# Wo in two parts: twelve split matmuls with the masked sums, the third modulation behind them, and w1's pieces split later

## The chip, the cores and the metric

The kernel runs on one core of one Trainium2 chip. The metric is the device time of one execution in microseconds (us). Before the change it is 433.62 us, the median of 3 runs (433.53 to 434.19).

A core has five engines, each of which works through its own list of instructions: TensorE (PE, matrix products, which write to PSUM), ScalarE (ACT), VectorE (DVE), GpSimd (POOL) and SyncE (SP). SP and POOL also issue transfers (DMA). In the profile, PEld is PE loading the stationary operand.

## What is computed

One block of a network over S = 2048 tokens of D = 448 channels: linear attention, then a mixer MLP over the tokens (F = 1792), each behind a layernorm that six vectors made from `c` modulate.

```python
x = A_x
mod = (_silu(c) @ w_mod).reshape(c.shape[0], 6, 1, -1)
sa, ca, ga, sb, cb, gb = (mod[:, 0], mod[:, 1], mod[:, 2], mod[:, 3], mod[:, 4], mod[:, 5])
h = _layernorm(x, axis=-1) * (1 + ca) + sa
x = x + ga * _A_ref(h, A_wqkv, A_wo)
h = _layernorm(x, axis=-1) * (1 + cb) + sb
x = x + gb * _B_ref(h, B_w1, B_b1, B_w2, B_b2)
```

Inside `_A_ref`, with 16 heads of 28 channels and `phi(t) = where(t > 0, t + 1, exp(t)) + 1e-6`:

```python
kv = jnp.einsum("bhsd,bhse->bhde", pk, v)
z = jnp.einsum("bhsd->bhd", pk)
num = jnp.einsum("bhqd,bhde->bhqe", pq, kv)
den = jnp.einsum("bhqd,bhd->bhq", pq, z)[..., None] + 1e-6
o = num / den            # then o, heads side by side, @ wo
```

The kernel multiplies kv by Wo before it meets the queries, so that per token only one product with a 448 x 448 matrix is left. `ga`, the third modulation vector (`mods[2]` in the code), scales the columns of that matrix.

## The kernel before

**Number format.** Most products are split: each operand is a high part, rounded to the format fp32r, and a low part, the rest. A product is then three fast matmuls: high x high, high x low and low x high. `split` (L82) makes the two parts with an ACT copy (L83) and a DVE subtraction (L84). A second way, used for some tiles, takes the subtraction off DVE: ACT copies the high part, ACT writes its negative into the low tile, and a transfer that adds, issued on POOL, puts the full value on top (`PIECE_DMA` pieces of w1 at L324 to L328; the keys' low part at L527 and L528). A few products are plain fp32 and not split: `kvb` (L818), the transposes (L863) and, before the change, Wo's product `wp` (L968).

**Order.** The schedule is written out by hand: every engine does its instructions in the order in which the code issues them, and a wait blocks what stands behind it on that engine. Tiles come from pools of buffers (`slot`: 74; `tslot`: 27; PSUM: 8 banks), and a new tile waits until the last user of its buffer is done.

**First loop** (L682 to L780, turns t = 4 to 15, one token tile of 128 rows each): keys of tile t on PE (`kp`), their exp and relu on ACT (L446, L449), `pk` on DVE (L458). `pk` of the tile before is cut into `pkh` (ACT, L515) and `pkl`; for tiles 13 to 15 `pkl` comes from DVE (L525), and `pk` is added to a running sum (L534). The normed x of one or two tiles (`HIGH_AT`) is made on DVE (`xn`, L496) and cut into `xh` (ACT, L500) and `xl` (DVE, L505, L506). PE adds the outer product of tile t - 4 into four banks `cacc` (L554), eleven matmuls a tile; the last four tiles follow behind the loop (L789 to L796). In turns 10 to 14 some query tiles are projected too (`qp`, `eq`, `rq`, `pq`). At the end of turns 13, 14 and 15 DVE multiplies parts 0, 1 and 2 of Wo (112 rows each) by `mods[2]` (L779); part 3 follows at L791.

**Behind the loop:** the sum of `pk` is closed (L784), cut into `zh` and `zl` (L786), and summed over the partitions on PE (`zp`, L799); ACT copies it to `zb`. `split_to(n)` cuts w1's pieces up to n, 0 to 7, at L794 (to 2), L803 (4), L812 (6) and L825 (8), all by `split`. From `cacc` and `zb` come four tiles `csum` (ACT L808, DVE L809). PE multiplies them with Wv (`kvb`, L818, 16 small fp32 matmuls, 32 records), DVE masks the heads' blocks (`kvm`, L822), and PE projects one more query tile (L962). Meanwhile DVE makes the denominators of tile 0: `b_prod`, `b_sum`, `b_eps` (POOL), `b_recip`, `b_scale` (L963).

**Wo's product** (L966 to L977): for each of four groups g of 112 channels one fp32 matmul of `kvm`'s columns with Wo's part g, an ACT copy out of PSUM (`wpg`, L970), and transfers that bring the rows to tiles of 128 (`Wpr`, L977). `wp_split` (L980) cuts those into `Wph` and `Wpl`.

**Second loop** (L988 to L1072): in turn i PE transposes the scaled queries of tile i (`tq`, L863), multiplies those of tile i - 1 by `Wph` and `Wpl` (`op`, L893, L900), and from turn 5 on adds up the mixer's first product (`up`, L950 to L952), which uses piece k of w1 from turn k + 5 on. Turn 0 projects three query tiles (`QS`). At the end of each turn `split_to` cuts more pieces, and `split_end` (L315) issues the adding transfers that wait. Behind it lies the rest of the MLP, which the change doesn't touch.

Of the kernel before, what the change touches and what calls it, by code (L numbers as in the profile page):

```python
# [16 lines left out]
NT = S // P  # L17
# [3 lines left out]
DH = 28  # L21
EPS = 1e-5

PIECE_DMA = range(8, 18)
PRE_LOAD = {14: 2, 15: 4}
KV_LAG = 4
HIGH_AT = {13: (11, 12), 14: (13,), 15: (14, 15)}
# [10 lines left out]
CUT2 = {2: 9, 3: 9, 4: 8, 5: 7}  # L38
LAG = 5
MOD_AT = {11: [(4, 0), (4, 1), (4, 2)], 13: [(4, 3), (4, None), (3, 0), (3, 1)]}  # L40
QS = {0: 3}
WARM = 6
POOL_LOW = (0, 1, 2)
# [8 lines left out]
def block_kernel(ctx: ExitStack, tc: tile.TileContext, x, xt, wqkv, wo, w1, b1, w2, c, wmod, wfirst, out):  # L52
# [19 lines left out]
    def tslot(name, dt=F32, parts=P, w=D):  # L72
        return tok.tile([parts, w], dt, name=name, tag="tok", padded_shape=[P, 512])


    def moving(new, name, dt=F32R, parts=P):
        return new(name, dt=dt, parts=parts, w=512)[:, 16:16 + D]

    def bank(name):
        return psum.tile([P, 512], F32, name=name, tag="bank")  # L80

    def split(full, hi, lo):  # L82
        nc.scalar.activation(hi, full, AF.Copy)  # L83
        nc.vector.tensor_sub(lo, full, hi.bitcast(F32))  # L84
# [400 lines left out]
    def a_phi_q(keep=0):  # L485
        a_exp_q(keep)
        for t in sorted(eqs):
            pq[t] = phi_q(t)
# [28 lines left out]
    def a_pk_parts(t):  # L517
        if t not in pks:
            a_pk_high(t)
        a_pk_low(t)  # L520
# [156 lines left out]
    low()  # L677
    sum_end()
    a_split(7)
    wo_sb = []  # L680
    late = [t for t in range(NT) if t not in Q_EARLY.values()]
    for t in range(4, NT):  # L682
        if 5 < t < NT - 1:
            project(t + 1, 1, "kp")
        kp = close(t, 1) if t > 4 else kps[4]
        if t == 9:
            row_sum(0)
            row_bias(0)
        if t > 4:
            a_outer(t - KV_LAG)  # L690
        if t % 2 and 4 < t < NT - 2:
            a_transpose(t + 1)
# [24 lines left out]
        a_pk_parts(t - 1)  # L717
        highs = HIGH_AT.get(t, (t - 2,))
        for i in highs[:1]:
            a_norm(i)  # L720
            a_high(i)
        if t % 2 == 0 and 4 < t < NT - 3:
            low = a_rows(t + 2)
        if t == 11:
            low2 = mod_high(2)
        for j, i in MOD_AT.get(t, ()):
            mod_add(j) if i is None else mod_part(j, i)
        if t == 14:
            low4()
        a_pk(t, kp)  # L730
        if t % 2 == 0 and 4 < t < NT - 3:
            low()
        if 7 < t + 3 < NT:
            a_split_low(t + 3)
        for i in highs[1:]:
            a_norm(i)
            a_high(i)
        if pair:
            first(1)
        for i in highs:  # L740
            a_low(i)
        if pair:
            second(1)
            end()
        sum_end()
        if 4 <= t < 8:
            w_high(0, t - 4)
            if t == 7:
                w_row(0)
        if t == 9:  # L750
            row_out(0)
        if t == 12:
            mod_out(2, mp)
            make_mask()
        if t in FETCH:
            load_xt(FETCH[t])
            load_x(FETCH[t])
        if 7 <= t < 11:
            mod_part(2, t - 7)
        if t == 10:  # L760
            mod_add(2)
        if t == 11:
            low2()
        if t == 13:
            low4 = mod_high(4)
        if t in (7, 10):
            load_mod(4 if t == 7 else 3)
        if t == 10:
            load_qkv(2, tslot)
        if t == 8:  # L770
            for g in range(4):
                w = tslot(f"wo{g}", parts=G)
                nc.sync.dma_start(w, wo[g * G:(g + 1) * G, :])
                wo_sb.append(w)
            b12 = cst.tile([P, NF + NT], F32, name="b12")
            nc.sync.dma_start(b12, b1)
            b1c, b2c = b12[:, :NF], b12[:, NF:]
        if t >= 13:
            nc.vector.tensor_mul(wo_sb[t - 13], wo_sb[t - 13], mods[2][:G])  # L779
        load_to(PRE_LOAD.get(t, 0))  # L780


    a_pk_parts(NT - 1)
    nc.vector.tensor_add(pksum[1], pksum[1], pksum[0])  # L784
# [12 lines left out]
    zp = bank("zp")  # L797
    for i, pk in enumerate(zs):
        nc.tensor.matmul(zp[:, :D], ones_r, pk, start=(i == 0), stop=(i == 1))  # L799
# [22 lines left out]
    nc.vector.tensor_mul(kvm, kvb[:G, :D], mask)  # L822
# [7 lines left out]
    pns, phs, ys, opb, sums, nms, nm2s, rss, vss = {}, {}, {}, {}, {}, {}, {}, {}, {}  # L830

    dens, prods, lasts = {}, {}, {}

    def b_prod(t):
# [13 lines left out]
    def b_scale(t):  # L848
        pn = pns.pop(t, None) or tslot(f"pn{t}", w=512)
        nc.vector.scalar_tensor_tensor(pn[:, :D].rearrange("p (h d) -> p h d", d=DH),  # L850
                                       pq[t].rearrange("p (h d) -> p h d", d=DH), 1e-6,
                                       dens.pop(t).unsqueeze(2).to_broadcast([P, H, DH]),
                                       op0=ALU.add, op1=ALU.mult)
        pns[t] = pn
        pq[t] = None

    def b_transpose(t):
        pn = pns.pop(t)
# [101 lines left out]
            del parts[k]  # L960

    a_q(late.pop(0))  # L962
    for fn in (b_prod, b_sum, b_eps, b_recip, b_scale):  # L963
        fn(0)
    mod_add(3)
    for g in range(4):  # L966
        wp = bank(f"wp{g}")
        nc.tensor.matmul(wp[:G, :D], kvm[:, g * G:(g + 1) * G], wo_sb[g], start=True, stop=True)  # L968
        wpg = tslot(f"wpg{g}", parts=G)
        nc.scalar.activation(wpg, wp[:G, :D], AF.Copy)  # L970
# [416 lines left out]
```

## Time and profile before

| what | value |
|---|---|
| median of 3 runs | 433.62 us (433.53 to 434.19) |
| the profiled execution | 434.09 us, its span 432.4 us |
| granted TensorE clock | 1.000 |
| PE busy | 427.9 us, 99% of the span |
| DVE busy | 365.1 us, 84% |
| ACT busy | 278.9 us, 65% |
| POOL busy | 120.1 us, 28% |
| Wo's product on PE (`wp`) | 3.01 us of the chain, from 108.81 us |

The span runs from the first to the last instruction on the core; the execution's own time is 1.7 us longer. A row of a timeline gives the start, the time from start to end, the engine, the line, the operation, the tile written and the tiles read, the shape and how many were merged; in brackets stands how long the engine had been idle and what ended that. Instructions of an engine overlap a little, so that one of 0.58 us can be followed by the next after 0.48. The ends of matmuls are modelled; their starts tell the rate. A row of the chain gives the start, the time on the chain, the engine, tile, line and count.

### The profile page before, as it was taken

The page shows a single profiled execution, that of the slowest core. Times are in us where ns is not written, and L with a number is a line of the kernel's source. Part 1 is how long each engine was busy: PE and PEld are TensorE (multiplying, and loading weights), DVE is VectorE, ACT ScalarE, POOL GpSimd, SP SyncE. Part 2 cuts the span into 40 slices and gives each one's busy share as a digit, 9 for nine tenths or more (in the row PEclk, how much of TensorE's full clock was granted, in tenths as well). Part 3 has the DMA queues.
Part 4 walks back from the last instruction along what each step waited for, and adds up shares of the span by engine and source line. Part 5 has one row for each costly group of instructions (what it writes and reads, how often), then busy time and mean ns, then how long its engine had stood idle before and what let it go on. Part 6 is the DMA issues. An engine that isn't in the chain of part 4 may idle for free.

```text
span 432.4 us, 7216 instructions
## 1 busy us (share of the span) xinstructions
PE 427.9 (99%) x2331; PEld 398.0 (92%) x2331; DVE 365.1 (84%) x814; ACT 278.9 (65%) x595; POOL 120.1 (28%) x199
## 2 busy tenths in 40 slices
PE   8999999999999999999999999999999999999997
PEld 8888899999899999999999999999999999999996
DVE  4899987889899999998579695739799998898894
ACT  5799869658578899996755263537464664655550
POOL 4345444300026577775200000010113131132010
PEclk9999999999999999999999999999999999999999
DMA  8997997565300036354427461577379977986431
GB/s 282 385 337 162 239 264 162 89 206 193 86 1 0 26 74 148 74 125 97 145 85 244 142 212 50 166 203 210 79 193 214 207 159 159 214 170 144 85 46 41
DMA packets 63797, 66.14 MB, mean 153 GB/s; under 512 B 4816, under 2 KB 55312, under 8 KB 63760
## 3 DMA queue, kind: packets, MB, share of 16 engines
q1 hardware_dynamic: 54688, 50.90, 37.8%
q0 software_dynamic: 8784, 14.32, 20.8%
q10 hardware_dynamic: 288, 0.46, 0.4%
q8 instruction: 18, 0.29, 0.3%
q14 instruction: 19, 0.16, 0.1%
HBM read 46.30 MB, written 7.34 MB: 124 GB/s over the span
## 4 chain that ended last, share of the span: by engine, by line
PE 97%; DVE 1%; ACT 1%; issue 0%
PE y L1183 19%; PE up L951 10%; PE up L950 10%; PE up L952 10%; PE y L1184 9%; PE cacc L554 7%; PE qp L432 7%; PE op L893 7%; PE kp L432 6%; PE op L900 1%; PE warm L188 1%; PE tq L863 1%; PE qp L439 1%; PE kvb L818 1%; PE wp L968 1%; PE rowb L287 1%
## 5 line engine op out<-in xcount | busy, mean ns | idle before, releaser
L950 PE MATMUL up<-h2h,ph 128*128 128x448 f32 x224 | 81.2, 362 | 0.0
L951 PE MATMUL up<-h2l,ph 128*128 128x448 f32 x224 | 81.2, 362 | 0.0
L952 PE MATMUL up<-h2h,pl 128*128 128x448 f32 x224 | 80.8, 361 | 0.0
L1138 POOL DMA_DIRECT2D a<-a x16 | 14.2, 964 | 142.6 <-DMA pr<-in_B_w_dram 76.7
L950 PEld LDWEIGHTS up<-h2h,ph 128*128 128x128 f32 x224 | 42.0, 188 | 3.1
L952 PEld LDWEIGHTS up<-h2h,pl 128*128 128x128 f32 x224 | 41.9, 187 | 3.0
L951 PEld LDWEIGHTS up<-h2l,ph 128*128 128x128 f32 x224 | 42.0, 188 | 2.3
L84 DVE TENSOR_TENSOR pl<-pr,ph 128x512 fp32r<-128x512 f32 x46 | 30.7, 688 | 2.6 <-ACT ph L83 1.7
L1189 ACT ACTIVATE cc<-y 128x448 f32<-128x448 f32 x24 | 13.0, 546 | 26.7 <-PE y L1184 26.7
L1102 DVE TENSOR_TENSOR u<-u,mod 128x448 f32<-128x448 f32 x14 | 8.7, 623 | 23.0 <-ACT u L1101 22.8
L83 ACT ACTIVATE ph<-pr 128x512 fp32r<-128x512 f32 x46 | 27.6, 623 | 0.8 <-PE up L952 0.5
L1101 ACT ACTIVATE u<-up,b 128x448 f32<-128x448 f32 x14 | 8.8, 625 | 25.4 <-PE up L952 24.9
L432 PE MATMUL kp<-wh,hh 128*128 128x448 f32 x64 | 23.8, 377 | 0.0
L554 PE MATMUL cacc<-pkh,xh 128*128 128x448 f32 x64 | 23.6, 369 | 0.0
L432 PE MATMUL qp<-wh,hh 128*128 128x448 f32 x64 | 23.5, 368 | 0.0
L1203 POOL DMA_DIRECT2D out_dram<-yt x14 | 12.7, 909 | 37.3 <-DVE yt L1194 27.9
L843 POOL TENSOR_SCALAR den<-den 128x16 f32<-128x16 f32 x16 | 8.8, 548 | 44.2 <-DVE den L840 44.2
L554 PE MATMUL cacc<-pkl,xh 128*128 128x448 f32 x56 | 20.3, 362 | 0.0
L893 PE MATMUL op<-wph,pth 128*128 128x448 f32 x48 | 18.7, 390 | 0.0
L1144 DVE TENSOR_TENSOR a<-a,s 128x512 f32<-128x512 f32 (+1 forms) x32 | 18.5, 622 | 0.0
L83 ACT ACTIVATE s2h<-s 128x512 fp32r<-128x512 f32 (+1 forms) x16 | 8.3, 569 | 15.5 <-DVE s L1144 15.5
L1183 PE MATMUL y<-ub,a11h 128*128 128x448 f32 x56 | 18.2, 375 | 0.0
(235 smaller groups left out, 1383.7 us busy)
## 6 DMA issues: line engine op xcount, KB each, us to landing
pr<-in_B_w_dram SPq DMA_DIRECT2D x56, 256.0 KB, 3.1
a<-in_B_w_dram SPq DMA_DIRECT2D x32, 256.0 KB, 4.8
a<-in_B_w_dram SPq DMA_DIRECT2D x32, 192.0 KB, 4.7
xt<-in_xt_dram SPq DMA_DIRECT2D x16, 256.0 KB, 5.0
x<-in_A_x_dram SPq DMA_DIRECT2D x16, 224.0 KB, 5.0
wm<-in_B_wmod_dram SPq DMA_DIRECT2D x16, 196.0 KB, 5.2
out_dram<-x SPq DMA_DIRECT2D x14, 224.0 KB, 2.3
out_dram<-yt POOLq DMA_DIRECT2D x14, 224.0 KB, 6.1
```

Source lines behind the costliest of these rows:

```text
L83: nc.scalar.activation(hi, full, AF.Copy)
L84: nc.vector.tensor_sub(lo, full, hi.bitcast(F32))
L432: nc.tensor.matmul(pps[t, j][:, :D], a[:, ch * P:(ch + 1) * P], w, start=first, stop=False)
L554: nc.tensor.matmul(cacc[ch][:, :D], a[:, s], b, start=(t == 0 and i == 0), stop=(t == NT - 1 and i == len(todo) - 1))
L893: nc.tensor.matmul(opb[t][:, :D], a, b, start=(ch == n == 0), stop=False)
L950: nc.tensor.matmul(ps[:, :D], hi[:, sl], mh, start=first, stop=False)
L951: nc.tensor.matmul(ps[:, :D], hi[:, sl], ml, start=False, stop=False)
L952: nc.tensor.matmul(ps[:, :D], lo[:, sl], mh, start=False, stop=last)
L1138: nc.gpsimd.dma_start(w, a, accum_op=ALU.add)
L1144: nc.vector.tensor_tensor(w, raw2[q, a][i], raw2[q, b][i], op=op)
L1183: nc.tensor.matmul(ps[:, :D], h[:, s], w, start=opens and r == 0, stop=False, skip_group_check=True)
L1184: nc.tensor.matmul(ps[:, :HD], l[:, s], wh, start=False, stop=closes and r == PAIRS - 1, skip_group_check=True)
```

## The change

Wo is no longer multiplied by `mods[2]` on the way in. Its four parts are cut into a high and a low tile by two activations on ACT and an adding transfer on POOL's queue, parts 0 and 1 at the end of turn 13, part 2 of turn 14 and part 3 of turn 15. `kvm` is cut as well (ACT and DVE). The four fp32 matmuls become twelve split ones, groups 0 and 1 taken in turns. DVE multiplies their results by `mods[2]` on the way out of PSUM, in place of ACT's copies.

The first tile's denominators move ahead of `kvm`, the helper functions with them. `mod_out(4)`, an ACT copy, moves ahead of `kvm`. Pieces 4 to 7 of w1 were cut at L812 and L825; now piece 4 is cut ahead of the twelve matmuls in the order of the code, piece 5 behind them, and pieces 6 and 7 at the end of turn 0 of the second loop, in the second way (two activations and a POOL transfer).

```diff
-PIECE_DMA = range(8, 18)
+PIECE_DMA = range(6, 18)
...
+WO_AT = {13: (0, 1), 14: (2,), 15: (3,)}
...
+    def wo_split(g):
+        full, hi, lo = wo_sb[g], moving(slot, f"woh{g}", parts=G), moving(slot, f"wol{g}", parts=G)
+        nc.scalar.activation(hi, full, AF.Copy)
+        nc.scalar.activation(lo, hi.bitcast(F32), AF.Copy, scale=-1.0)
+        nc.gpsimd.dma_start(lo, full, accum_op=ALU.add)
+        wos.append((hi, lo))
...
-        if t >= 13:
-            nc.vector.tensor_mul(wo_sb[t - 13], wo_sb[t - 13], mods[2][:G])
+        for g in WO_AT.get(t, ()):
+            wo_split(g)
         load_to(PRE_LOAD.get(t, 0))
...
-    nc.vector.tensor_mul(wo_sb[3], wo_sb[3], mods[2][:G])
...
     a_q(late.pop(0))
-    split_to(6)
+    b_prod(0)
+    b_sum(0)
+    b_eps(0)
     mp = mod_sum2(4)
...
     a_phi_q()
+    b_recip(0)
+    mod_out(4, mp)
     kvm = slot("kvm", parts=G)
     nc.vector.tensor_mul(kvm, kvb[:G, :D], mask)
-    mod_out(4, mp)
+    b_scale(0)
+    kvh, kvl = slot("kvh", dt=F32R, parts=G), slot("kvl", dt=F32R, parts=G)
+    split(kvm, kvh, kvl)
     load_to(PRE + MID + 3)
-    split_to(8)
...
     a_q(late.pop(0))
-    for fn in (b_prod, b_sum, b_eps, b_recip, b_scale):
-        fn(0)
     mod_add(3)
+    split_to(5)
+    wps = [bank(f"wp{g}") for g in range(4)]
+    for gs in ((0, 1), (2,), (3,)):
+        for i, (a, b) in enumerate(((kvh, 0), (kvh, 1), (kvl, 0))):
+            for g in gs:
+                nc.tensor.matmul(wps[g][:G, :D], a[:, g * G:(g + 1) * G], wos[g][b], start=(i == 0), stop=(i == 2))
     for g in range(4):
-        wp = bank(f"wp{g}")
-        nc.tensor.matmul(wp[:G, :D], kvm[:, g * G:(g + 1) * G], wo_sb[g], start=True, stop=True)
         wpg = tslot(f"wpg{g}", parts=G)
-        nc.scalar.activation(wpg, wp[:G, :D], AF.Copy)
+        nc.vector.tensor_mul(wpg, wps[g][:G, :D], mods[2][:G])
...
     low3 = mod_high(3)
+    split_to(6)
```

More of the change, by code (lines that the diff above doesn't have):

```diff
@@ L679, in block_kernel @@
     a_split(7)
-    wo_sb = []
+    wo_sb, wos = [], []
+    def wo_split(g):
[4 more added lines that the diff above has]
+        wos.append((hi, lo))
     late = [t for t in range(NT) if t not in Q_EARLY.values()]
@@ L777, in block_kernel, with b_prod, b_sum, b_eps @@
             b1c, b2c = b12[:, :NF], b12[:, NF:]
-        if t >= 13:
-            nc.vector.tensor_mul(wo_sb[t - 13], wo_sb[t - 13], mods[2][:G])
+        for g in WO_AT.get(t, ()):
+            wo_split(g)
         load_to(PRE_LOAD.get(t, 0))
+    pns = {}
+    dens, prods, lasts = {}, {}, {}
+    def b_prod(t):
+        prods[t] = tslot(f"pd{t}")
+        nc.vector.scalar_tensor_tensor(prods[t], pq[t], 1e-6, zb, op0=ALU.add, op1=ALU.mult)
+    def b_sum(t):
+        dens[t] = small.tile([P, H], F32, name=f"den{t}", tag="den")
+        nc.vector.tensor_reduce(dens[t], prods.pop(t).rearrange("p (h d) -> p h d", d=DH), axis=AX.X, op=ALU.add)
+    def b_eps(t):
+        nc.gpsimd.tensor_scalar_add(dens[t], dens[t], 1e-6)
+    def b_recip(t):
+        nc.vector.reciprocal(dens[t], dens[t])
+    def b_scale(t):
+        pn = pns.pop(t, None) or tslot(f"pn{t}", w=512)
+        nc.vector.scalar_tensor_tensor(pn[:, :D].rearrange("p (h d) -> p h d", d=DH),
+                                       pq[t].rearrange("p (h d) -> p h d", d=DH), 1e-6,
+                                       dens.pop(t).unsqueeze(2).to_broadcast([P, H, DH]),
+                                       op0=ALU.add, op1=ALU.mult)
+        pns[t] = pn
+        pq[t] = None
     a_pk_parts(NT - 1)
@@ L820, in block_kernel @@
     a_phi_q()
+    b_recip(0)
+    mod_out(4, mp)
     kvm = slot("kvm", parts=G)
     nc.vector.tensor_mul(kvm, kvb[:G, :D], mask)
-    mod_out(4, mp)
+    b_scale(0)
+    kvh, kvl = slot("kvh", dt=F32R, parts=G), slot("kvl", dt=F32R, parts=G)
+    split(kvm, kvh, kvl)
     load_to(PRE + MID + 3)
-    split_to(8)
     Wpr, Wph, Wpl = [], [], []
     H2h, H2l = [None] * NT, [None] * NT
-    pns, phs, ys, opb, sums, nms, nm2s, rss, vss = {}, {}, {}, {}, {}, {}, {}, {}, {}
-    dens, prods, lasts = {}, {}, {}
-    def b_prod(t):
-        prods[t] = tslot(f"pd{t}")
-        nc.vector.scalar_tensor_tensor(prods[t], pq[t], 1e-6, zb, op0=ALU.add, op1=ALU.mult)
-    def b_sum(t):
-        dens[t] = small.tile([P, H], F32, name=f"den{t}", tag="den")
-        nc.vector.tensor_reduce(dens[t], prods.pop(t).rearrange("p (h d) -> p h d", d=DH), axis=AX.X, op=ALU.add)
-    def b_eps(t):
-        nc.gpsimd.tensor_scalar_add(dens[t], dens[t], 1e-6)
-    def b_recip(t):
-        nc.vector.reciprocal(dens[t], dens[t])
[L848 to L855, printed above, removed]
+    phs, ys, opb, sums, nms, nm2s, rss, vss = {}, {}, {}, {}, {}, {}, {}, {}
     def b_transpose(t):
```

## The prediction

> **What bounds the kernel now.** I read the page first, its busy shares and the chain that ended last:
>
> ```profile
> PE   427.9 (99%) x2331; PEld 398.0 (92%) x2331; DVE 365.1 (84%) x814; ACT 278.9 (65%) x595; POOL 120.1 (28%) x199
> ...
> PE 97%; DVE 1%; ACT 1%; issue 0%
> ```
>
> TensorE (PE) is the chain almost from end to end, so the time moves only by what PE has more or less to do, and by new gaps in PE. Next I read the chain in order of time where the change sits:
>
> ```profile
> 98.82 2.00 PE qp L432 x10
> ...
> 106.58 2.02 PE qp L432 x10
> 108.60 0.20 PE qp L439
> 108.81 3.01 PE wp L968 x8
> 111.82 0.33 PE tq L863 x3
> ```
>
> PE runs from one group into the next. The four products with Wo (`wp`, eight records) take 3.01 us, and the next group starts the moment they end. A split matmul of the same 448 columns (`qp`) takes 2.00/10 = 0.20 us.
>
> Third, the timelines of PE, ScalarE (ACT) and VectorE (DVE) from 80 to 99 us, the last turns of the loop over the token tiles (t = 13, 14, 15). First ACT:
>
> ```profile
> 80.01 0.58 ACT L515 ACTIVATE pkh<-pk 128x448 fp32r<-128x448 f32 x1
> 80.62 0.58 ACT L527 ACTIVATE pkl<-pkh 128x448 fp32r<-128x448 f32 x1
> 81.11 1.03 ACT L500 ACTIVATE xh<-xn 128x448 fp32r<-128x448 f32 x2
> ...
> 82.50 0.62 ACT L465 ACTIVATE eq<-qp,mv 128x448 f32<-128x448 f32 x1
> ...
> 84.57 0.58 ACT L515 ACTIVATE pkh<-pk 128x448 fp32r<-128x448 f32 x1
> 86.80 0.58 ACT L500 ACTIVATE xh<-xn 128x448 fp32r<-128x448 f32 x1 [1.65 <-DVE xn L496]
> 87.28 0.62 ACT L465 ACTIVATE eq<-qp,mv 128x448 f32<-128x448 f32 x1
> ...
> 89.36 0.59 ACT L515 ACTIVATE pkh<-pk 128x448 fp32r<-128x448 f32 x1
> 91.66 0.58 ACT L500 ACTIVATE xh<-xn 128x448 fp32r<-128x448 f32 x1 [1.71 <-DVE xn L496]
> 92.61 0.58 ACT L500 ACTIVATE xh<-xn 128x448 fp32r<-128x448 f32 x1 [0.38 <-DVE xn L496]
> 93.10 0.56 ACT L515 ACTIVATE pkh<-pk 128x448 fp32r<-128x448 f32 x1
> 96.28 0.58 ACT L83 ACTIVATE zh<-pk 128x448 fp32r<-128x448 f32 x1 [2.62 <-PE cacc L554]
> ```
>
> ACT idles 1.65 + 1.71 + 0.38 + 2.62 = 6.36 us here, and the last turn's `zh` waits too. DVE shows what these waits are:
>
> ```profile
> 85.18 0.63 DVE L525 SCALAR_TENSOR_TENSOR pkl<-pk,pkh 128x448 fp32r<-128x448 f32 x1 [0.88 <-ACT pkh L515]
> ...
> 86.26 0.51 DVE L496 TENSOR_SCALAR xn<-x,mv 128x448 f32<-128x448 f32 x1
> ...
> 89.98 0.62 DVE L525 SCALAR_TENSOR_TENSOR pkl<-pk,pkh 128x448 fp32r<-128x448 f32 x1 [0.24 <-ACT pkh L515]
> ...
> 92.57 0.55 DVE L506 TENSOR_TENSOR xl<-xn,xh 128x384 fp32r<-128x384 f32 x1
> ...
> 93.84 0.62 DVE L779 TENSOR_TENSOR wo<-wo,mod 112x448 f32<-112x448 f32 x1
> 94.37 0.62 DVE L525 SCALAR_TENSOR_TENSOR pkl<-pk,pkh 128x448 fp32r<-128x448 f32 x1
> ...
> 95.56 0.63 DVE L784 TENSOR_TENSOR pk<-pk,pk 128x448 f32<-128x448 f32 x1
> 96.89 0.63 DVE L84 TENSOR_TENSOR zl<-pk,zh 128x448 fp32r<-128x448 f32 x1 [0.70 <-ACT zh L83]
> ```
>
> The two engines pass one chain back and forth: `pkh` on ACT ends 84.57 + 0.58 = 85.15, DVE's `pkl` starts at 85.18, `xn` ends 86.77, ACT's `xh` starts at 86.80. ACT's idle time is DVE working on what ACT gave it; it isn't spare. Last, what PE asks for:
>
> ```profile
> 93.86 0.36 PE L554 MATMUL cacc<-pkh,xh 128*128 128x448 f32 x1
> ...
> 94.26 0.36 PE L554 MATMUL cacc<-pkh,xl 128*128 128x448 f32 x1
> ...
> 96.26 0.36 PE L554 MATMUL cacc<-pkl,xh 128*128 128x448 f32 x1
> ...
> 98.46 0.36 PE L799 MATMUL zp<-zl,ones_r 128*128 128x448 f32 x1
> ```
>
> `xh` of tile 14 is there at 91.66 + 0.58 = 92.24 and taken at 93.86: slack 1.62. Its `xl`, ready at 93.12, is taken at 94.26: slack 1.14. `pkl` of tile 15, ready 94.99, taken 96.26: 1.27. `zl`, ready 97.52, taken 98.46: 0.94. These four slacks decide the case.
>
> **The change, part by part.**
>
> *Twelve matmuls for four.* Each split matmul is put at 0.20 us, the `qp` step (same 448 columns, 112 rows instead of 128), so 12 x 0.20 = 2.4 us for 3.01: PE has 0.6 us less. The bounds are 0.20 and the old record's 3.01/8 = 0.376 us, which gives 4.5 us and a loss of 1.5; I take 0.20, since each split group of this width in the chain steps so. The Trainium skill (FP8 and Floating Point Precision, section TensorE Precision Notes) counts four passes for a true FP32 product; sixteen passes against twelve would save, as an estimate, 4 x 0.20 = 0.8 us instead, while the trace has eight records of 0.376 us.
>
> *Wo's parts.* Eight activations, in pairs: a high part, and a negated copy of it that must wait for it. The same pair stands at 80.01 and 80.62, and the next instruction starts at 81.11: 1.10 us a pair. Two pairs stand behind turn 13 (before the `eq` at 82.50), one behind turn 14 (before the `eq` at 87.28), one behind turn 15 (before the `pkh` at 93.10). Each is last in its turn, so all of the next turn's ACT work is queued behind it. The four adding transfers go out on POOL's queue:
>
> ```profile
> 109.78 0.29 POOL L843 TENSOR_SCALAR den<-den 128x16 f32<-128x16 f32 x1 [26.39 <-DVE den L840]
> ```
>
> POOL is idle for 26.39 us up to that point, and the parts are wanted at 108.8: nothing.
>
> How far that pushes things: the chain of turn 14 starts 2.2 us late, and so does turn 15's, with 1.1 more: 3.3 us. Every link down to `xh` of tile 14 waits on ACT, so all of it passes on.
> - `xh` of tile 14: 92.24 + 3.3 = 95.54, PE wants it at 93.86: late by 1.7.
> - `xl` of tile 14: 93.12 + 3.3 = 96.42, wanted at 94.26: late by 2.2.
> - `pkh` of tile 15, with the fourth pair: 93.10 + 4.4 = 97.50, ends 98.06. DVE has lost its product with Wo (93.84) and starts `pkl` at once, 98.10 to 98.72, wanted at 96.26: late by 2.5.
> - The sum of `pk` (L784) starts 95.56 - 94.37 = 1.19 behind that `pkl`: 99.29, ends 99.92; `zh` starts 0.09 later as now, 100.01; `zl` 0.61 behind it, 100.62, ends 101.25, wanted at 98.46: late by 2.8.
>
> The lateness doesn't add up, for each stall of PE postpones the next demand; the largest, 2.8 us, is what PE has lost when `zp` ends. Nothing behind gives it back, since PE is without gaps from there on. Bounds of a pair: below, 0.96 us, two steps of 0.48 as between `xh` at 86.80 and the `eq` at 87.28, which makes the last item 2.8 - 4 x 0.14 = 2.2; above, a part's buffer that isn't free when ACT comes to it. No row shows that; with the shortest wait of ACT above, 0.38 us, at each of the four pairs it would be 2.8 + 1.5 = 4.3. I keep 1.10, the rows of the same operation.
>
> *DVE's four products with Wo removed* (0.62 us each, L779 and L791): one of them is the 0.5 us already used above; the others stood beside waits. Nothing more.
>
> *The masked sums' split.* `kvm` becomes `kvm`, `kvh` (ACT), `kvl` (DVE), with the old first-tile steps ahead:
>
> ```profile
> 106.68 0.63 DVE L822 TENSOR_TENSOR kvm<-kvb,mask 112x448 f32<-112x448 f32 x1 [0.24 <-issue]
> 107.22 1.28 DVE L84 TENSOR_TENSOR pl<-pr,ph 128x512 fp32r<-128x512 f32 x2
> ...
> 110.40 0.62 DVE L850 SCALAR_TENSOR_TENSOR pn<-pq,den 128x448 f32<-128x448 f32 x1
> ```
>
> PE covers this with a projection, 106.58 to 108.81. `kvm` ends 107.31, `kvh` (0.58) about 107.95, so 0.85 us of slack. `kvl`, behind the scaling (0.62), ends about 108.6, and the first matmul with it is the fifth, wanted at 109.6. Ahead of `kvm` DVE loses the low parts of pieces 4 and 5 (1.28 us for two) and gets the first tile's product and sum (0.62 each, as the scaling) and a small reciprocal, which waits for POOL's 0.29: by my estimate up to 0.4 us later against PE, and slack is left in both: nothing. Without that cover it would cost what is over, up to 1.2 us for the two steps.
>
> *The third modulation on DVE* instead of ACT's copies. DVE takes 0.63 us from PSUM (`kvm`'s row) against this:
>
> ```profile
> 109.60 0.55 ACT L970 ACTIVATE wpg<-wp 112x448 f32<-112x448 f32 x1 [2.45 <-PE wp L968]
> ...
> 114.92 1.16 DVE L84 TENSOR_TENSOR wpl<-wpr,wph 128x448 fp32r<-128x448 f32 x2 [0.28 <-ACT wph L83]
> ...
> 119.26 0.37 PE L893 MATMUL op<-wpl,pth 128*128 128x448 f32 x1
> ```
>
> The results leave perhaps 1 us later, behind `mod_add`, one piece's low part and each other. The first use of `wpl` is at 119.26 and it is ready near 115.5: 3.7 us of slack, nothing.
>
> *Pieces of w1.* Pieces 4 and 5 go from before `kvm` to around `wp`; 6 and 7 to the end of turn 0 of the second loop, by two activations each and a POOL transfer. Piece k is first used in turn k + 5, far off. Four activations of about 0.58 us, 2.3 us, then stand in front of turn 1, where ACT now waits:
>
> ```profile
> 119.25 0.49 ACT L871 ACTIVATE pth<-tq 128x384 fp32r<-128x384 f32 x1 [1.63 <-PE tq L863]
> ```
>
> The 0.7 us over goes into `pth`, whose next use on PE is a turn later: nothing.
>
> **Sum.** +2.8 - 0.6 = +2.2 us. The profiled execution took 434.09 us (a span of 432.4, and 1.7 around it), 0.47 over the median; on it 436.3, on the median of 433.62 it is **435.8 us**, 0.5% slower.
>
> **Rivals.**
>
> *The eight activations hide* (not slower). If ACT could put them into its 6.36 us of idle time, of which they need 4.4, PE sees nothing and the time is 433.62 - 0.6 = 433.0. For it: the totals. Against it: the waits are links of one chain, and ACT takes its instructions as written. It decides at 1.14 us, the slack of `xl` of tile 14: pairs that push it by less cost nothing there. The Trainium skill (PSUM — Partial Sum Buffer, section Engine vs sequencer instructions) calls ScalarE's and VectorE's queues strict FIFO; by that rule this rival falls, and the rows of 85 to 87 us, where ACT waits for `xn` with later work at hand, agree. Chance 0.13.
>
> *The masked sums come late as well.* If DVE is 1 us further behind than I count, `kvh` misses `wp` by 0.6: 436.4. For it: DVE is the busiest helper (84% on the page), and its two rows at 106.68 and 107.22 follow each other without a gap. Against: the slack of 0.85. Chance 0.12.
>
> *The split products aren't short* (the change doesn't do what it says): 0.376 us each, 435.8 + 2.1 = 437.9. Against it: every such row here. Chance 0.02.
>
> **How the numbers follow.** The forecast has 0.70; 0.03 remains for something that I don't see and that is faster. The range takes the low bound of a pair (2.2 - 0.6 = +1.6, 435.2), the second rival and most of the way to the buffers' bound (437.3), with half a microsecond below for slack that I read too small: 434.7 to 437.2. It leaves out the first rival and the third. 0.2% is 0.87 us, about what a measurement of this kernel can tell from no change. The first rival, at -0.14%, is "same", less a little for the case that part of the stall is left: same 0.13, slower 0.84, faster 0.03.
>
> **What would show it.** Right: PE idle before the `cacc` matmuls of tiles 14 and 15 and before `zp`, released by DVE's `xl`, `pkl` and `zl`, 2.8 us together; `zp` near 101.2 instead of 98.4; ACT's `eq` of turn 14 near 84.7 and of turn 15 near 90.6; twelve `wp` matmuls in 2.4 us, with no wait before them. Wrong: `cacc` without gaps up to `zp`, the new activations lying in ACT's old idle times, or a stall at `wp` larger than the one at `cacc`.

## The result, and the profile after

The changed kernel takes 441.5 us (median of six runs, 440.23 to 442.36) against 433.82 for the kernel before on the same chip: a ratio of 1.0176, interval 1.0157 to 1.0195. Slower, as forecast, but by 7.7 us where 2.2 was forecast, and outside the range. Two executions of the experiments below, at a granted clock of 0.558 (705.59 us, in e8) and 0.757 (526.34 us, in e18), are left out. The profiled execution took 440.93 us, with a span of 439.2. Its page, busy shares and the chain that ended last:

```profile
PE 429.1 (98%) x2335; PEld 395.7 (90%) x2335; DVE 364.1 (83%) x813; ACT 283.7 (65%) x602; POOL 126.0 (29%) x205
...
PE 76%; ACT 7%; DVE 7%; DMA 7%; issue 2%; POOL 0%; SPq 0%; ACTq 0%; DVEq 0%; POOLq 0%
```

PE is busy for 1.2 us more than before, and the span is 6.8 us longer: nearly all of the loss is waiting. The chain, 97% PE before, now runs through ACT, DVE and DMA for 21%. Where PE waits stands in its timeline (start, duration, engine, line, operation; in brackets the idle time ahead of it and what ended it):

```profile
95.50 0.47 PE L555 MATMUL cacc<-pkh,xh 128*128 128x448 f32 x1 [1.92 <-ACT xh L501]
...
96.39 0.47 PE L555 MATMUL cacc<-pkh,xl 128*128 128x448 f32 x1 [0.21 <-DVE xl L507]
...
101.37 0.37 PE L433 MATMUL qp<-wh,hh 128*128 128x448 f32 x1
...
107.22 2.61 PE L854 MATMUL kvb<-cs,wr 128*112 128x112 f32 x24 [0.24 <-DVE cs L843]
...
112.67 0.66 PE L983 MATMUL wp<-woh,kvh 112*112 112x448 f32 x2 [0.62 <-ACT kvh L84]
...
115.19 0.49 PE L877 MATMUL tq<-ident,pn 128*128 128x128 f32 x3
...
128.59 0.44 PE L914 MATMUL op<-wph,pth 128*128 128x448 f32 x1 [1.76 <-ACT rq L467]
...
129.47 0.55 PE L877 MATMUL tq<-ident,pn 128*128 128x128 f32 x3 [0.23 <-DVE pn L811]
...
134.97 0.63 PE L877 MATMUL tq<-ident,pn 128*128 128x128 f32 x4 [0.33 <-DVE pn L811]
```

The reader is to see four places, not one: at `cacc` (token tiles 14 and 15, behind the loop), from `kvb` to `wp`, at the late product of the second loop (L914, the last quarter of a tile's product with Wo, called the late `op` below), and at the transposes `tq` behind it.

The moment at which a kernel reaches this stretch differs between the traces: the query projection ahead of the last K tile starts at 84.83 us before, at 84.01 to 85.08 in three traces of the changed kernel, and at 83.77 to 85.70 in all. So all times below are counted from that projection, and given as their difference to the kernel before. The third row is a later execution of the changed kernel, not edited:

| us behind the kernel before | projection behind `zp` | projection behind `kvb` | `wp` | first `tq` | late `op` | first `up` | end |
|---|---|---|---|---|---|---|---|
| before, absolute | 13.83 | 21.52 | 23.82 | 26.82 | 38.24 | 57.67 | 347.57 |
| changed | +3.15 | +3.69 | +4.46 | +3.98 | +5.96 | +7.34 | +7.24 |
| changed, e13 | +2.74 | +3.27 | +4.03 | +3.58 | +4.00 | +5.39 | +5.35 |

From the first `up` on hardly anything is lost or won (0.1 us). ScalarE's timeline has the start of it; the single row below it is `cs` in the kernel before, without a wait:

```profile
82.47 0.56 ACT L685 ACTIVATE woh<-wo 112x448 fp32r<-112x448 f32 x1
83.07 0.58 ACT L686 ACTIVATE wol<-woh 112x448 fp32r<-112x448 f32 x1
...
84.63 0.62 ACT L466 ACTIVATE eq<-qp,mv 128x448 f32<-128x448 f32 x1
...
90.50 0.62 ACT L466 ACTIVATE eq<-qp,mv 128x448 f32<-128x448 f32 x1
...
103.79 0.64 ACT L842 ACTIVATE cs<-cacc,col 128x448 f32<-128x448 f32 x1 [0.64 <-PE qp L440]
...
105.81 1.68 ACT L842 ACTIVATE cs<-cacc,col 128x448 f32<-128x448 f32 x3 [1.38 <-PE qp L433]
...
112.04 0.58 ACT L84 ACTIVATE kvh<-kvm 112x448 fp32r<-112x448 f32 x1 [2.01 <-DVE kvm L860]
```

```profile
100.34 2.21 ACT L808 ACTIVATE cs<-cacc,col 128x448 f32<-128x448 f32 x4
```

`eq` of turn 14 starts at 84.63 (forecast 84.7) and of turn 15 at 90.50 (90.6). But `cs`, which reads only finished sums, waits for PE's query projections, first for 0.64 and then for 1.38 us. An instruction that doesn't read `qp` and waits for it is waiting for a buffer: in the built program `cs` got buffers of the split query tiles 5 and 6, which the projections were still reading; in the kernel before, the first three got buffers of K's last tile.

### The profile page after: what moved, and what is told of

Read it like the earlier page. It is cut to its first block, busy times and chain, and to the rows that moved or that the text cites. A ratio compares the mean times of both kernels' runs of the same rounds, so it can differ in the third digit from the quotient of the medians.

```text
span 439.2 us, 7243 instructions
## 1 busy us (share of the span) xinstructions
PE 429.1 (98%) x2335; PEld 395.7 (90%) x2335; DVE 364.1 (83%) x813; ACT 283.7 (65%) x602; POOL 126.0 (29%) x205
## 3 DMA queue, kind: packets, MB, share of 16 engines
HBM read 46.30 MB, written 7.34 MB: 122 GB/s over the span
## 4 chain that ended last, share of the span: by engine, by line
PE 76%; ACT 7%; DVE 7%; DMA 7%; issue 2%; POOL 0%; SPq 0%; ACTq 0%; DVEq 0%; POOLq 0%
PE y L1200 19%; PE up L965 10%; PE up L964 10%; PE up L966 10%; PE y L1201 9%; PE op L907 5%; PE cacc L555 3%; PE kp L433 2%; DMA xt<-in_xt_dram 2%; DMA wr<-in_qkv_dram 2%; PE qp L433 2%; DMA pk<-pk 2%; PE op L914 1%; PE tq L877 1%; DMA wpr<-wpg 1%
## 5 line engine op out<-in xcount | busy, mean ns | idle before, releaser
L85 DVE TENSOR_TENSOR pl<-pr,ph 128x512 fp32r<-128x512 f32 x44 | 29.4, 686 | 2.7 <-ACT ph L84 1.7
L84 ACT ACTIVATE ph<-pr 128x512 fp32r<-128x512 f32 x44 | 26.5, 619 | 0.8 <-PE up L966 0.5
```

## The experiments

Ratios are to the kernel before, timed beside each on the same chip (medians 433.39 to 433.87).

**e1, Wo's parts in turns 10 and 12.** `-WO_AT = {13: (0, 1), 14: (2,), 15: (3,)}` `+WO_AT = {10: (0, 1), 12: (2, 3)}`.

> The changed kernel with Wo's parts cut at the ends of turns 10 and 12 instead of 13 to 15, where ScalarE next waits for PE's transposes (3.4 and 2.9 us). Theory (separate delays: 2.7 us by the eight activations in the chain up to zp, the rest by buffers and by the pieces' activations): zp is back near 98.5 us, the csum tiles still wait for the projection whose operands held their buffers, the late op of tile 0 stays: 441.5 - 2.7 = 438.8 us (438.0 to 439.5). Rival (the buffers alone make the time, the activations' delay would have been taken up by what waits for buffers): no change, 440.5 to 442.

440.28 us, 1.0141 [1.0110, 1.0173]; 1.5 above the 438.8 and 0.8 above the range. The projection behind `zp` is 0.49 late instead of 2.74 to 3.15, but PE waited 1.06 us earlier in the loop (at 64.95), and all later terms stayed. Ahead of that, ScalarE's second low part had waited 2.38 us for a transfer of `pk`, which it doesn't read: in the built program its buffer was that of an earlier `pk`.

**e2, pieces 6 and 7 split in turns 2 and 3.** `-split_to(8 + max(0, i - 5))` `+split_to(6 + min(2, max(0, i - 1)) + max(0, i - 5))`.

> The changed kernel with pieces 6 and 7 of w1 cut at the ends of turns 2 and 3 of the second loop instead of both at the end of turn 0. Theory: their four activations stood in front of pth of tile 1 and held PE's last op of tile 0 for 1.9 us, and what followed was late with it; without them 441.5 - 1.9 to - 3.2 = 438.3 to 439.6 us. Rival (the late landing of Wpr's rows holds PE): PE waits as before, 441 to 442 us.

439.56 us, 1.0136 [1.0116, 1.0155]: at the upper end of what was expected. The wait at the late `op` fell from 1.8 to 1.1, not to nothing: the slowest transfer of `wpr` landed 4.0 us after its issue (2.6 before), so the rival had a part in it too.

**e3, the parts alone in the kernel before.** Eight activations and four transfers at the change's places, in buffers of the pool, kept until `wp`; the data are those of the modulation vector instead of Wo's. No product reads them: eight small VectorE writes ahead of `wp`, 0.2 us together and behind the steps shown below, end their use. All else is as before.

```diff
+        for g in {13: (0, 1), 14: (2,), 15: (3,)}.get(t, ()):
+            wo_split(g)
```

> The kernel before with one addition, whose results nobody multiplies with: eight activations and four adding transfers of the shapes of Wo's parts (cut from the third modulation vector's tile), in the same places and with the same eight buffers, each touched by one small VectorE write ahead of wp, which ends its use. Theory: 2.7 us at zp plus 0.5 to 1.3 us behind it by the csum tiles' buffers: 433.8 + 3.2 to + 4.0 = 437.0 to 437.8 us. Rival (buffers cost nothing by themselves): 436.5. Rival (the stall at zp is of another part of the change): 433.8.

443.59 us, 1.0226 [1.0211, 1.0241]: 5.8 above the range, and slower than the whole change. VectorE's and PE's timelines:

```profile
114.75 0.69 DVE L84 TENSOR_TENSOR pl<-pr,ph 128x512 fp32r<-128x512 f32 x1 [2.54 <-PE wp L981]
```

```profile
118.11 0.88 PE L873 MATMUL tq<-ident,pn 128*128 128x128 f32 x3 [3.46 <-DVE pn L860]
```

The low part of a piece of w1, which has nothing to do with `wp`, waits for `wp`: in the built program its buffer is that of `kvm`, which PE reads. All of the first tile's steps on VectorE stand behind it, and `tq` waits 3.46 us. Eight buffers held longer, and the losses turn up in three other places: 0.5 us at `kvb`, 0.6 at `wp`, 3.7 at `tq`.

**e4, the same with three tiles of its own.** `+own = [cst.tile([G, D], F32R, name=f"own{i}") for i in range(3)]`, and the parts go there.

> The same addition to the kernel before, but into three tiles of its own, so that no buffer of the pool is taken. Theory: only the 2.7 us at zp are left, 436.5 us (436.2 to 436.9), and the csum tiles don't wait for PE. Rival (buffers make most of it): 434 to 435.

437.36 us, 1.0078 [1.0060, 1.0096]; 0.9 above the 436.5, 0.5 above the range. PE waits only at `cacc` (1.65 and 0.22), is 2.89 us behind after `zp` and 2.99 at the first `up`. So the activations by themselves cost 2.9, and the buffers most of the 6.2 us between e3 and e4. In the two traces 7.3 us lie between them at the first `up`, 2.7 of it from the first `tq` to the late `op`, where nothing waits and PE's clock is halved (last section).

**e5, fewer loads ahead.** The changed kernel, and w1's pieces loaded later, which leaves buffers free: `-load_to(10)` `+load_to(5)`, `-load_to(14)` `+load_to(6)`, `-load_to(PRE + MID + 3)` `+load_to(8)`.

> The changed kernel with fewer of w1's pieces loaded ahead: up to 5, 6 and 8 behind the first loop instead of 10, 14 and 17, so that nine buffers stay free; in the built program the csum tiles then wait for no projection. Theory (buffers): csum and kvh are on time, only the activations' delay up to zp (2.7 to 3.5 us) and perhaps part of the late op of tile 0 are left, less the 0.5 us of the shorter products: 436.0 to 437.5 us. Rival (the buffers only stood beside another wait): 440 to 441.5.

439.58 us, 1.0141 [1.0121, 1.0161]: 2.1 above the range, but the mechanism showed. In the built program the first three `cs` get the buffers of K's last tile again, and `wp` is at +2.79 instead of +4.46, with no wait at `kvb` or `wp`. The wait at the late `op`, 1.84, stayed, with a landing of 4.0.

**e6, e5 and e2 together.**

> As the run with fewer loads, and pieces 6 and 7 cut at the ends of turns 2 and 3 as well. Theory: what is left is the delay of the eight activations less the shorter products, 433.8 + 3.0 - 0.5 = 436.3 us (435.8 to 436.8), with no wait of PE behind zp. Rival: a wait in the second loop stays, 437 to 439.

437.31 us, 1.0088 [1.0065, 1.0111], 0.5 above the range. `wp` +2.76, first `tq` +2.20, no wait at the late `op`, first `up` +3.08: behind `zp` a wait of 0.32 at `tq` stayed, against the expectation.

**e7, e6 and Wo's parts behind turn 15.** `WO_AT = {}`; parts 0 and 1 behind K's last split, 2 behind `split_to(2)`, 3 behind `split_to(4)`.

> As the run before it (fewer loads, pieces 6 and 7 later), and Wo's parts cut where ScalarE has nothing in its chain: parts 0 and 1 behind the last pkh, ahead of zh (2.6 us idle in the kernel before), part 2 behind pieces 0 and 1, part 3 behind pieces 2 and 3. Theory: all three delays are gone and only the shorter products are left: 433.8 - 0.5 = 433.3 us (433.0 to 433.9). Rival (the split of the masked sums or the evacuation by VectorE has a cost of its own): 434.3 or more.

435.46 us, 1.0037 [1.0023, 1.0051]: the rival. First `tq` is at -0.35, so the shorter products pay; then 0.7 us of wait at the late `op` and two at `tq`, and the first `up` is at +1.90.

**e8, the same move of the parts alone.**

> The changed kernel with only Wo's parts moved, to the same places behind the last pkh; the loads and pieces 6 and 7 as changed. Theory: the 2.7 to 3.5 us of the activations are gone, the csum tiles' buffers and the late op of tile 0 stay: 441.5 - 3.1 = 438.4 us (437.6 to 439.2). Rival (the buffers' waits take the place of the activations' delay): 440 to 441.5.

436.08, 437.61 and 438.93 us, 1.0089 [1.0064, 1.0115]: the middle one is at the lower end of what was expected. No trace of these three was kept, so where their time went wasn't seen.

**e9, e10, e11: VectorE's work around `wp`.** On e7: e9 multiplies Wo by the third modulation vector on VectorE ahead of the parts (`-nc.vector.tensor_mul(wpg, ..., mods[2][:G])` `+nc.scalar.activation(wpg, ..., AF.Copy)`); e10 splits pieces 4 to 7 in turns 2 to 5; e11 does both.

> The kernel with all three edits, and Wo multiplied by the third modulation vector on VectorE ahead of its parts, as the kernel before did (one 0.55 us product each in turns 13, 14, 15 and behind the loop), so that the four evacuations of wp are ScalarE copies again and VectorE enters the second loop without four products of 0.55 us. Theory (the 2.2 us between the first output product, 0.8 us early, and the first up-projection, 1.4 us late, in the kernel with all three edits come from VectorE's evacuation of wp together with pieces 4 and 5, which make the normalised tiles late): half or more of it goes, 433.6 to 434.6, the waits of tq for pn go and the first up-projection starts at most 0.6 us late. Rival 1 (it comes from the transfers of wpr and the split of the fourth one, which start as late here): no change, 435.0 to 436.0. Rival 2 (the products in front of the parts put VectorE late at the transposes of K's last tiles): zp 0.5 us or more later than in the kernel with all three edits, 435.5 to 436.5.

> The kernel with all three edits, and pieces 4 and 5 of w1 split in turns 2 and 3 of the second loop and 6 and 7 in turns 4 and 5, with the parts' second half by transfer (pieces 4 and 5 were split around the wp products, with VectorE's subtraction of 0.68 us each); VectorE's evacuation of wp stays. Theory (VectorE's work around wp makes the normalised tiles late): 1.4 us of VectorE's 3.6 us goes, so 434.0 to 435.0, first up-projection up to 1 us late. Rival 1 (the transfers of wpr are what is late): no change, 435.0 to 436.0. Rival 2 (ScalarE's two more pairs in turns 2 and 3 hit pth there): waits of op for pth in turns 2 and 3, 435.5 to 437.

> The kernel with all three edits, with the factor in front on VectorE and pieces 4 to 7 later: VectorE has none of the four products and none of the two subtractions around wp. Theory: the 2.2 us goes wholly, first up-projection 0.5 to 1.0 us earlier than in the kernel before, 432.6 to 433.4, which beats both kernels. Rival 1 (transfers of wpr): 434.8 to 435.8. Rival 2 (ScalarE's four copies and its later pairs): waits of op for pth, 434 to 436.

e9: 433.40 us, 0.9993 [0.9984, 1.0002], 0.2 below what was expected and no difference to the kernel before that can be measured; first `tq` -0.34, first `up` -0.15. e10: 435.53, 1.0040 [1.0028, 1.0053], its first `up` at -0.09 in the trace, yet the time is the rival's. e11: 434.21, 1.0010 [1.0001, 1.0019]: missed, by a wait of 0.5 at the late `op`. My theory gave no reason for e11 to be worse than e9. The traces did: in e7 and e11 one transfer of `wpr` lands late (3.6 and 4.2 us after its issue), in e9 and e10 none does.

**e12, e13: the changed kernel again, twice; e14, e15: e7 and e9 again.** No edit.

> The changed kernel once more, nothing edited. In its first trace one of the eight transfers of wpr landed 3.8 us after its issue (2.0 to 2.6 in the trace of before), wph of the fourth part waited 2.17 us for it, and the four activations of pieces 6 and 7 stood behind that; the wait in front of the late output product was 1.8 us. Theory (the late landing belongs to single executions, as in six of the ten traces read so far): the slowest landing may be anything from 2.6 to 4 us, and the wait follows it, 0.2 to 0.5 us with 2.6 and 1.8 with 3.8. Rival (it belongs to the kernel, by where its buffers lie or by what else is moved): 3.8 and 1.8 again.

> As the run before it: the changed kernel once more. Theory (single executions): a landing of 2.6 in one of the two, and then at most 0.5 us of wait before the late output product. Rival (the kernel): 3.8 and 1.8 in both.

> The kernel with all three edits once more. In its first trace the slowest landing was 3.6 us, the fourth wph started at 119.03 behind a wait of 2.04 us, and the late output product waited 0.7 us. Theory (single executions): with a landing of 2.6 the wait before the late output product is 0, and the first up-projection comes 0.7 to 1.4 us earlier against its first projection than in the first trace (59.57 us after the first query projection shown); with 3.6 it is the same again. Rival (the kernel): 3.6 and 0.7 again.

> The kernel with all three edits and the factor in front, once more. In its first trace the slowest landing was 2.5 us and no wait stood before the late output product. Theory (single executions): it may show a landing of 3.6 to 4 now, and then a wait of about 0.5 us before the late output product. Rival (the kernel, or ScalarE's copies keep the transfers apart): 2.5 and no wait again.

One run of each: 441.15, 439.70, 436.75 and 434.27 us. The slowest landing was 4.2, 2.6, 4.3 and 2.6 us, the wait at the late `op` 2.21, 0.28, 1.35 and nothing. The late landing belongs to single executions. ScalarE in the changed kernel, first trace and e13:

```profile
123.60 0.58 ACT L84 ACTIVATE wph<-wpr 128x448 fp32r<-128x448 f32 x1 [2.17 <-DMA wpr<-wpg]
124.08 0.62 ACT L327 ACTIVATE ph<-pr 128x512 fp32r<-128x512 f32 x1
...
126.45 0.47 ACT L885 ACTIVATE pth<-tq 128x384 fp32r<-128x384 f32 x1
```

```profile
122.33 0.58 ACT L84 ACTIVATE wph<-wpr 128x448 fp32r<-128x448 f32 x1 [0.64 <-DMA wpr<-wpg]
122.82 0.62 ACT L327 ACTIVATE ph<-pr 128x512 fp32r<-128x512 f32 x1
...
125.19 0.47 ACT L885 ACTIVATE pth<-tq 128x384 fp32r<-128x384 f32 x1
```

`wph` waits for the transfer, the four activations of pieces 6 and 7 follow, and `pth` stands behind them. The releaser that the timeline names for the late `op`, ScalarE's `rq`, misleads: it runs from 127.92 to 128.55, just ahead of the product, which doesn't read it. The built program has the product wait for the last part of `pth`, which VectorE writes:

```profile
128.15 0.61 DVE L899 TENSOR_TENSOR pth<-tq,pth 64x128 fp32r<-64x128 f32 x2
```

Now the DMA view of 120.6 to 124 us, again the first trace and then e13 (the window in 40 slices; then the queue named instruction, packets, MB, share):

```profile
GB/s 316 190 190 42 63 361 295 148 274 211 106 0 21 0 0 0 0 0 0 0 21 0 21 0 21 0 21 0 0 0 0 0 0 0 0 0 0 0 0 0
...
q8 instruction: 1, 0.02, 2.4%
```

```profile
GB/s 190 232 211 295 211 190 21 85 190 253 190 295 253 85 42 193 0 0 0 0 0 0 0 0 0 0 0 0 0 0 0 0 0 0 0 0 0 0 0 0
...
q8 instruction: 1, 0.02, 2.0%
```

In the first, almost all of the last transfer is through after 11 of the 40 slices; then four packets come singly (the last four 21s). The packets' own times: the instruction queue's packet of 16 KB runs from 121.04 to 122.32, and the four start at 122.31, 122.50, 122.69 and 122.87. In e13 it starts at 121.90, and the last packet of `wpr` had started at 121.84. Of the 19 traces (all but e8's), eight land late (3.6 us or more), and in all eight the four last packets start as that packet ends; in the other eleven (2.6 or less) it starts behind the start of the transfer's last packet, or isn't near.

**e16, e17, e18: the packet moved.** `keep_warm(7)` makes dummy matmuls at the start; 1 in e16 (on the changed kernel) and e17 (on e7), 11 in e18 (on e9).

> The changed kernel with twelve warm-up matmul records fewer at the start (they feed no result; the second warm-up call makes 1 product instead of 7). In all sixteen traces the queue named instruction moves one packet of 16 KB about every 125 matmul records, for 0.9 to 1.6 us; where that packet overlaps the last transfer of wpr, that transfer's last four packets start when it ends, and where it lies behind them the transfer lands in 2.6 us or less. Theory (the packet comes at a place in PE's instruction stream; twelve records fewer ahead of it put it twelve records, 2.4 us, later against the work): the slowest landing of wpr is 2.6 or less, the wait before the late output product 0.3, first up-projection about 63.1 us behind the first query projection shown at 84 to 85 us (65.0 in the first trace, 63.1 in the third), time 439.3 to 439.9 with a narrow spread. Rival 1 (the overlap is only coincidence): landings of 3.6 or more again in about half the executions, 440.2 to 442.4 as before. Rival 2 (the warm-up is needed): a lower granted clock or a later start at the beginning, time above 441.5.

> The kernel with all three edits (435.46, its two traces both with a late landing, 1.9 and 3.4 us lost up to the first up-projection) and twelve warm-up records fewer. Theory: the landing is on time, no wait before the late output product, first up-projection at most 0.3 us later than in the kernel before, measured from the first query projection (57.67 us there), time 433.4 to 434.2. Rival 1 (VectorE's evacuation of wp is what costs the 1.9 us, as I had it two calls ago): no change, 435.0 to 436.0, with waits of tq for pn. Rival 2 (coincidence): 435.0 to 436.0 with late landings.

> The kernel with all three edits and the factor in front (433.4, landing on time in both traces, the instruction packet 1.2 and 0.9 us behind the last packets of wpr) and eight warm-up records more (11 products instead of 7), which puts the packet about 1.6 us earlier against the work, onto the last transfer. Theory: the last transfer lands 3.3 to 4.3 us after its issue, its wph waits 1.5 us or more, and the late output product waits 0.2 to 1.2 us (ScalarE had 0.85 us of slack there), time 434.0 to 435.5. Rival (coincidence): landing of 2.6 or less, 433.2 to 434.0.

e16: 440.30 us, 1.0154 [1.0137, 1.0170]. The packet comes at 130.1, some 8 us later against the transfers than in the other traces of this kernel, where 2.4 was reckoned; the slowest landing is 2.6 and the wait at the late `op` 0.31. The time is 0.4 above what was expected; this trace ran part of the `cacc` stage at half clock (last section). e17: 434.90, 1.0034 [1.0022, 1.0046]: packet at 123.5, again 6 us or more later, landing 2.6, no wait at the late `op`, first `up` +0.60 instead of +1.90. The expected 434.2 was missed, for a wait of 0.33 at `tq` stays. e18: 434.65 (median of nine), 1.0018 [1.0005, 1.0030]; it says nothing on the landing, for the packet didn't move (it starts 1.0 us behind the start of the transfer's last packet, 1.15 in e9). That its time lies in the expected range is luck: the landing took 2.6, and the first projection comes 1.42 us later than in e9 (85.64 against 84.22), ahead of all that was to be tested. So the packet's place doesn't follow the count of matmuls as the theory had it; what sets it is open.

## Why the prediction was wrong

**Right: the eight activations.** Forecast 2.8 us at `zp`; 2.74 or 2.75 in the traces of e2, e5, e6, e12 and e13, 3.15 in the first, 3.97 in e16 at half clock. Without them there (e7) it is 0. The step at `cacc`, with ACT and DVE in one chain, held as worked out: `xh`, `xl`, `pkl` and `zl` let PE go on 2.08, 2.57, 2.79 and 3.05 us late in the first trace, where 1.7, 2.2, 2.5 and 2.8 stood. The rival that they hide fell.

**Right in size: the products.** Forecast -0.6; `wp` to `tq` gave -0.45 to -0.48, since the first two matmuls of the group take 0.50 us (112.67 to 113.17) and the next two 0.41.

**Wrong: "a part's buffer that isn't free when ACT comes to it."** I asked only what buffers the new tiles would get, and kept it as an upper bound. The new tiles got theirs at once; the tiles behind them paid: `cs` waits for the projections, `kvb` is 0.5 late and `kvh` another 0.8, +1.3 at `wp` where "slack is left in both: nothing" stood. Shown by e5 and e6 (0.05 and 0.01 with fewer loads ahead), e4 (0.02 with tiles of its own) and e3 (1.08).

**Wrong: "the 0.7 us over goes into `pth`, whose next use on PE is a turn later: nothing."** The last columns of `pth` are made for a pair of tiles in the odd turn, and the late `op` of the even tile wants them at the start of the next turn. The rows are the late `op` before and in e13, and the fourth `wph` before:

```profile
123.07 0.36 PE L900 MATMUL op<-wph,pth 128*128 128x448 f32 x1
```

```profile
127.32 0.44 PE L914 MATMUL op<-wph,pth 128*128 128x448 f32 x1 [0.28 <-ACT rq L467]
```

```profile
117.05 0.58 ACT L83 ACTIVATE wph<-wpr 128x448 fp32r<-128x448 f32 x1 [0.66 <-DMA wpr<-wpg]
```

Before, 3.82 us lay between `pth` (119.25) and the late `op`; in e13 it is 2.13 (125.19 to 127.32), as in the first trace, which is what the steps between them need, so 1.7 was slack. The next table has the starts against the first `tq`, in traces where every landing took 2.6 us or less:

| us behind the first `tq` | before | e13 | e6 | e17 | e9 | e10 |
|---|---|---|---|---|---|---|
| first transfer of `wpr` issued | -1.45 | 0.02 | -0.06 | 0.12 | -0.60 | -0.59 |
| fourth `wph` | 5.40 | 6.85 | 6.86 | 6.91 | 6.16 | 6.22 |
| `pth` of turn 1 | 7.60 | 9.71 | 7.64 | 7.64 | 7.59 | 7.65 |
| lost from the late `op` to the first `up` | 0 | 1.39 | 0.85 | 0.92 | 0.21 | 0.20 |

From the fourth `wph` to `pth` it is 2.86 us in e13 against 2.20: the 0.7 of the forecast, and by itself it would have fitted into the 1.7. But the fourth `wph` is 1.45 late too, for the results of `wp` leave later; the forecast had 1 us for that and held it against `wpl` alone. Together `pth` is 2.1 late, and 0.4 reaches PE. The later results alone cost nothing at the late `op` (e6, e17: no wait there); the four activations alone weren't run. In the first trace it is 1.98, for the late landing comes on top: before, ACT had 1.63 us idle ahead of `pth` that would have taken it, and the change filled that time. That before would have hidden a late landing is argued from that row, not shown.

**Wrong: "3.7 us of slack, nothing" for the third modulation on DVE.** The slack was that of the first `wpl` at `op`. The path that counts runs from the results through the transfers and the fourth `wph` to VectorE, where the next tile's `pn` stands behind the fourth `wpl` and the steps on `pth`, and `tq` waits for `pn`. From the late `op` to the first `up` it costs 1.38 us in the first trace and 1.39 in e13. VectorE isn't short of time there, it waits (e13):

```profile
122.94 0.63 DVE L85 TENSOR_TENSOR wpl<-wpr,wph 128x448 fp32r<-128x448 f32 x1 [0.59 <-ACT wph L84]
...
126.13 0.56 DVE L892 TENSOR_TENSOR ptl<-tq,pth 128x384 fp32r<-128x384 f32 x1 [0.84 <-ACT pth L888]
```

With pieces 6 and 7 later the second wait is gone, and 0.85 (e6) and 0.92 (e17) are left. With the products off VectorE (e9), or without piece 4's low part ahead of them (e10), the transfers leave some 0.7 us earlier, and 0.2 is left: either edit is enough while the landing is on time. In e11, with both edits and a landing of 4.2, it is 1.38 again.

**The sum.** e13: 2.74 + 1.29 - 0.45 + 0.42 + 1.39 = 5.39. The first trace: 3.15 + 1.31 - 0.48 + 1.98 + 1.38 = 7.34. The terms are the activations, the buffers, the products, the late `op` and the wait for `pn`. The forecast had the first and third, and put the others at nothing.

**Open.** e10's median is 2.1 us above e9's, and its trace only 0.5 behind the first projection; 2.0 to 2.1 us of each of its runs lie outside the span, against 1.7 in e9's, and its traced execution (434.97) is the fastest of the five. e17's median is 1.5 above e9's, its trace 0.7, and its traced execution (434.17) is the fastest of six. Whether the others had late landings wasn't seen. Nor was a landing made late by an edit: in e16 and e17, one trace each, it is on time with the packet away, and e18, which was to show the other side, didn't move it. e9 and e15, the same kernel, differ by 0.96 us, 0.93 of it ahead of the first projection; what happens there wasn't looked at.

## What to carry to other kernels

A tile that lives longer is paid for by the tiles that come after it: ask of each new buffer which later tile loses its free one, and whose reader that tile then waits for; the sign in a timeline is an instruction that waits for an engine whose output it doesn't read. An edit costed at "nothing" needs the next reader of what it delays followed down to PE, in that turn, and two edits that use the same slack have to be costed together: here 0.7 and 1.45 us, each inside 1.7, became a wait. Where a term swings between executions, profile the same kernel again before looking for its cause in the code.

## What was not expected of the hardware

**A fetch of instructions goes with a late transfer.** The 16 KB packet came 18 times in the trace of before, about every 130 matmul records, and took 0.9 to 1.4 us. In the eight late landings it took 0.9 to 1.6 us, and the transfer's last four packets started as it ended, 0.2 us apart; the landing was 1.0 to 1.7 us late. The traces don't name a packet's DMA engine: that the four stood behind the 16 KB on one engine is inferred from these times. The Trainium skill (Runtime: NRT & Kernel Launch, section Instruction fetch mechanics) says that an engine's sequencer fetches its program in blocks of 16 KiB over a DMA queue of its own, the cost mostly hidden; the size agrees, and in these eight traces the cost wasn't hidden.

**PE's clock halved behind some short waits.** In e12, behind the wait of 2.21 us at the late `op` (windows: the stretch and its length, the busy time of PE, PEld, DVE, ACT and POOL, and the granted clock, the DMA share and GB/s):

```profile
126.00:128.20 2.20, 0.06 (x1) 0.09 (x1) 1.30 (x5) 2.16 (x7) 1.53 (x3) 1.00 0.00 0
128.20:130.00 1.80, 1.56 (x6) 1.19 (x7) 1.71 (x4) 1.80 (x4) 0.58 (x1) 0.67 0.91 154
130.00:132.00 2.00, 2.00 (x7) 1.74 (x7) 2.00 (x6) 1.77 (x5) 0.02 (x1) 0.50 0.72 124
132.00:133.00 1.00, 1.00 (x6) 0.95 (x5) 0.97 (x3) 0.45 (x1) 0.52 (x1) 0.89 0.00 0
```

By these shares the clock is halved for 3.4 us, from about 0.7 us behind the end of the wait, and the matmuls step at 0.375 us instead of 0.20. The same follows a wait of 1.69 in e16, one of 1.35 in e14 and, for twice as long, the 3.46 us of e3. Besides the waits, by the times of the nearest trace without it, it costs 0.6 us from the late `op` to the first `up` in e12 (2.02 against 1.39 in e13), 0.8 in e14 (2.16 against 1.39 in e7) and 1.0 up to `zp` in e16 (3.97 against 2.74, the wait 0.2 longer). It didn't follow the waits of 1.92 and 1.76 in the first trace, nor those of 1.84 in e5 and 1.88 in e1; what decides isn't shown. Four of the changed kernel's six runs had a mean clock of 0.992 to 0.996, and they are the four longest (441.24 to 442.36, against 440.23 and 440.93). The Trainium skill (TensorE: Matmul & The Clock Gate, section What's actually happening) has the clock halved after an idle window of about 3.4 us that runs freely. The length of the halved stretch agrees; three of these four waits were shorter than that window. Each of the three has a second wait of 0.2 us a few matmuls behind it, but so have both waits of the first trace.
